# A first feed-forward turn split into token halves, with earlier loads of chunks and weights

## The chip, the cores and the metric

The kernel runs on one NeuronCore of a Trainium2 chip. The time is that of one execution on the device in microseconds (us); of several runs the median counts. A second path for inputs out of range (`slow`) is in the program and is skipped by a flag.

## What is computed

```python
f = 1.0 / (1.0 + np.exp(-f_logit))
for t in range(S):
    state = f[:, :, t, :, None] * state + np.einsum('bhd,bhe->bhde', k[:, :, t], v[:, :, t])
    y[:, :, t] = np.einsum('bhd,bhde->bhe', q[:, :, t], state)
```

In short: a gated linear attention over 4 sequences of 768 tokens with 8 heads of 48 (`state = f * state + k v`, `y = q state`); its output `x` (3072 tokens of 384) goes through `h = max(x @ w_in, 0)` and `(h * h) @ w_out`, with 2048 hidden units; and that through a soft mixture of 8 experts with 32 slots: logits `x @ phi`, a softmax over the tokens that gathers the slots, two layers per expert, and a softmax over the slots that gives the tokens back.

## The kernel before, in words

**Tiles.** The attention works on 24 chunks of 128 tokens, six to a sequence. Each chunk has a part that needs no matmul, `prep` (L142 on: the running product `ip` of the gates by four scans at L162, then `k` at L171 and `q` at L179 in that scale), and a part on PE, `chunk`: four transposes (`knat`, L193), the scores (L205) with their masks `a` (L208), the state sums (L220) with the state adds `S` (L226, L228), and the values (L243 from the state, L250 from the scores) with `y` (L254 to L259). Six small DMAs write `y` into `x` (L265, L268). A chunk is five steps of a generator, `stream`; `upto(n)` runs it to step n, so that 20 steps are a block of 512 tokens.

**Feed-forward.** Six blocks of 512 tokens go through 16 weight tiles `ff` of 128 hidden units each. For a pair (block, ff), `layer1` makes nine matmuls (three per 128 rows of the model, L118 to L120, since each operand is split into a high and a low part for one-pass products), then relu, square (L369 to L372) and the remainder `gl` on DVE (L374); `layer2` makes nine more into three banks `o`. The order of pairs is written out by hand: `TURNS` pairs blocks 0 and 1 so that weights can be split while they arrive: block 0 with tiles 0 to 3, block 1 with 0 to 8, block 0 with 4 to 15, block 1 with 9 to 15; then blocks 2 to 5 with all tiles. Between turns `put_by` saves the sums (L405, L407).

**The first turn** (block 0, tiles 0 to 3) does not split: `layer1_whole` and `layer2` use whole float weights and the whole `x`, in matmuls that the trace shows as two instructions each (L353, L384). It starts after step 23 (`FIRST`) and goes on to step 40, the end of block 1's attention; `x` of block 0 must be complete, that is, chunk 3 done.

**Weights.** `w_load` (L305) loads one tile as 64-bit numbers, 768 KB; `w_split` makes a float of it: two passes on ACT (L315, L319), a shift and a combine on DVE (L320, L321) and a last pass (L331 into `wn` for a whole tile, else L333 into `whi`); `w_parts` then splits it into high (ACT, L113) and low (DVE, L114). `x_split` does the same with `x`, by thirds of 512 columns. `WAHEAD` is the number of tiles loaded ahead.

**Queues.** All DMAs are issued by SP in one order (`g<-fkq` L136, `v` L138, `raw` L305, `x<-y`). The order on each engine is set ahead of time by the framework's scheduler from the order of the program and its priorities; each engine then goes through its list in order.

Of the kernel before, what the change touches and what calls it, by code (L numbers as in the profile page):

```python
# [18 lines left out]
HR = 64  # L19
# [38 lines left out]
class K:  # L58
# [173 lines left out]
    def values(self, i):  # L232
# [27 lines left out]
        if c == 0:  # L260
            self.x_alloc(b)
        xl = self.x[b][1].bitcast(F32)
        ts = slice(c * C, (c + 1) * C)
        for h in range(2):
            nc.sync.dma_start(out=xl[h * D : h * D + D, :, ts], in_=y[h * HR : h * HR + D, :KT])  # L265
        for h in range(2):
            for e, n, kt, o in PLACE[6 + h]:
                nc.sync.dma_start(out=xl[o : o + n, kt, ts], in_=y[h * HR + e : h * HR + e + n, KT])  # L268

# [20 lines left out]

    def x_split(self, b, kt):
        xh, xl = self.x[b]
        self.hl(xh[:, kt], xl[:, kt], xl[:, kt].bitcast(F32))

# [51 lines left out]

    def layer1_whole(self, b, ff):

        nc, fp = self.nc, self.fp
        x, w = self.x[b][1].bitcast(F32), self.whole[ff]  # L350
        o = self.ps.tile([128, 512], F32, tag="h", name="ph", bufs=2)[:, :TB]
        for kt in range(KT):
            nc.tensor.matmul(out=o, lhsT=w[:, kt * 128 : kt * 128 + 128], rhs=x[:, kt], start=kt == 0, stop=kt == KT - 1)  # L353
        r = fp.tile([128, TB], F32, tag="r", name="r", bufs=1)
        nc.scalar.activation(r, o, AF.Relu)
        g = fp.tile([128, TB], F32, tag="gl", name="g2", bufs=2)
        nc.scalar.activation(g, r, AF.Square)
        return g, None

    def layer1(self, b, ff):  # L360
        nc, fp = self.nc, self.fp
        x, w = self.x[b], self.w[ff]
        ph = self.ps.tile([128, 512], F32, tag="h", name="ph", bufs=2)
        o = ph[:, :TB]
# [4 lines left out]
        nc.scalar.activation(r, o, AF.Relu)  # L369
        gh = fp.tile([128, TB], F32R, tag="gh", name="gh", bufs=2)  # L370
        nc.scalar.activation(gh, r, AF.Square)  # L371
        nc.scalar.activation(r, r, AF.Square)  # L372
        gl = fp.tile([128, TB], F32R, tag="gl", name="gl", bufs=2)
        nc.vector.tensor_tensor(gl, r, gh.bitcast(F32), ALU.subtract)  # L374
        return gh, gl

    def layer2(self, b, ff, g, start, stop):

        if start:
            self.o[b] = [self.ps.tile([128, 512], F32, tag=f"o{t}", name=f"o{t}", bufs=1) for t in range(KT)]  # L380
        if g[1] is None:
            w = self.whole[ff][:, DM:]
            for t in range(KT):
                self.nc.tensor.matmul(out=self.o[b][t][:, :TB], lhsT=w[:, t * 128 : (t + 1) * 128], rhs=g[0], start=start, stop=stop)  # L384
            return
# [310 lines left out]
    def fast_blocks(self, main, pst, ast, wst, raw):  # L696

        def stream():
            for i in range(2):
                yield from self.prep(i)  # L700
            for i in range(NCH):
# [17 lines left out]

        st = stream()  # L720
        for _ in range(8):
            next(st)
        done = 0
        end = NCH * STEPS
# [6 lines left out]

        steps = [(b, ff) for b, f0, f1 in TURNS for ff in range(f0, f1)]
        paired = len(steps)
        steps += [(b, ff) for b in range(2, NB) for ff in range(NFF)]
# [5 lines left out]
        def target(n, b, ff):  # L740
            if n < n0:
                return min(2 * blk, max(FIRST, blk + (ff + 2) * blk // n0))
            if n < n1:
# [5 lines left out]
        def split(b):  # L749
            if b in unsplit:  # L750
                for kt in range(KT):
                    self.x_split(b, kt)
                unsplit.remove(b)

        def begin1(b, ff):
            if b == 0 and ff < WHOLE:
                return self.layer1_whole(b, ff)
            split(b)
# [6 lines left out]

        upto(FIRST)
        unsplit = list(ORDER)
        self.w_split(0, raw[0], True)
        wn = 1
        posts = iter(())  # L770
        pend = begin1(0, 0)
        wait = 0
        for n, (b, ff) in enumerate(steps):
            if n == 3:
                self.consts3()
            if wn < WHOLE or WHOLE <= n and wn < NFF:
                while len(raw) < min(NFF, wn + WAHEAD):
                    more_w()
                self.w_split(wn, raw[wn], wn < WHOLE)
                wn += 1  # L780
# [5 lines left out]
            nxt = None  # L786
            if n + 1 < len(steps):
                nxt = begin1(*steps[n + 1])
                if n0 <= n + 2 < n1:
                    part(steps[n + 2][1])  # L790
            upto(target(n, b, ff))
# [47 lines left out]
    def slow(self):  # L839
# [3 lines left out]
        with ExitStack() as main:  # L843
# [13 lines left out]
            with ExitStack() as st:  # L857
                self.pp = self.pool(st, "pp2")
                for b in range(NB):
                    self.x_alloc(b)  # L860
                    xh, xl = self.x[b]
                    self.hl(xh, xl, xT[:, :, b * TB : (b + 1) * TB])
                    for ff in range(NFF):
# [122 lines left out]
```

## Time and profile before

| | |
|---|---|
| median of 3 runs | 604.34 us (602.19 to 605.6) |
| profiled execution | 606.27 us, span 604.5 us |
| PE / DVE / ACT busy | 95% / 54% / 52% of the span |
| PE's mean granted clock | 0.989 |
| share of the chain of waits | PE 77%, DVE 7%, DMA 6%, ACT 6% |

Busy shares are means over stages. A row of an engine's list gives start and duration, and an idle time before it with the engine or DMA that ended it. [...]

### The profile page before, as it was taken

The numbers are of one execution on the slowest core, as the hardware profiler recorded it, in microseconds if no ns is written. First come the engines' busy times: TensorE is split into PE (matmuls) and PEld (weight loads), VectorE is DVE, ScalarE is ACT, GpSimd is POOL, SyncE is SP. The second block draws the span as 40 slices with busy tenths as digits, with TensorE's granted clock in tenths as the row PEclk, the third lists the DMA queues.
The fourth block names the chain that finished last, engine by engine and source line by source line (L and its number), as shares of the span: only waits on it lengthen the run. The fifth ranks groups of instructions, "written<-read, shape, count | busy, mean of one in ns | idle before, by whom it ended". The sixth has DMA issues, their size and how long they took to land.

```text
span 604.5 us, 13326 instructions
## 1 busy us (share of the span) xinstructions
PE 574.9 (95%) x5587; PEld 442.4 (73%) x5587; DVE 328.7 (54%) x688; ACT 314.8 (52%) x577; POOL 4.0 (1%) x10
## 2 busy tenths in 40 slices
PE   4899899999999999999999999999999999998993
PEld 3784467788787878778877777887788887886372
DVE  6978989999825547454464552543332322213322
ACT  5647759996635546354455354544334544442122
POOL 0000000000000000000000000000000100000000
PEclk9999979999999999999999999999999999999898
DMA  9557558421321202202211210220000745554757
GB/s 290 181 154 236 160 190 287 151 67 47 105 60 40 73 2 73 59 16 73 73 46 28 74 63 18 79 79 3 15 14 12 263 135 177 168 199 157 262 205 272
DMA packets 28324, 69.59 MB, mean 115 GB/s; under 512 B 4464, under 2 KB 17008, under 8 KB 28256
## 3 DMA queue, kind: packets, MB, share of 16 engines
q1 hardware_dynamic: 28256, 68.65, 35.8%
q8 instruction: 46, 0.75, 0.5%
q14 instruction: 22, 0.18, 0.1%
HBM read 59.20 MB, written 4.72 MB: 106 GB/s over the span
## 4 chain that ended last, share of the span: by engine, by line
PE 77%; DVE 7%; DMA 6%; ACT 6%; issue 2%; SPq 1%; ACTq 0%; DVEq 0%
PE o L118 10%; PE ph L118 9%; PE o L120 9%; PE ph L120 9%; PE ph L119 9%; PE o L119 9%; DMA g<-fkq 4%; PE psm L243 3%; DMA raw<-w 2%; DVE ip L162 2%; PE hp L591 2%; PE psm L220 2%; PE psm L205 2%; PE so L615 2%; PE o L384 1%
## 5 line engine op out<-in xcount | busy, mean ns | idle before, releaser
L374 DVE TENSOR_TENSOR gl<-r,gh 128x512 fp32r<-128x512 f32 x92 | 63.5, 690 | 119.2 <-ACT r L372 118.6
L369 ACT ACTIVATE r<-ph 128x512 f32<-128x512 f32 x92 | 54.7, 595 | 119.9 <-PE ph L120 114.9
L118 PE MATMUL o<-gh,w 128*128 128x512 f32 x276 | 112.8, 409 | 0.0
L118 PE MATMUL ph<-x,w 128*128 128x512 f32 x276 | 111.5, 404 | 0.0
L119 PE MATMUL o<-gh,w 128*128 128x512 f32 x276 | 108.0, 391 | 0.0
L120 PE MATMUL o<-gl,w 128*128 128x512 f32 x276 | 106.3, 395 | 1.8 <-DVE gl L374 1.7
L120 PE MATMUL ph<-x,w 128*128 128x512 f32 x276 | 107.8, 391 | 0.0
L119 PE MATMUL ph<-x,w 128*128 128x512 f32 x276 | 107.6, 390 | 0.0
L120 PEld LDWEIGHTS o<-gl,w 128*128 128x128 f32 x276 | 51.6, 188 | 15.7 <-DVE gl L374 4.8
L118 PEld LDWEIGHTS ph<-x,w 128*128 128x128 f32 x276 | 51.8, 188 | 14.7 <-issue 4.1
L118 PEld LDWEIGHTS o<-gh,w 128*128 128x128 f32 x276 | 51.7, 187 | 12.6 <-ACT gh L371 0.5
L120 PEld LDWEIGHTS ph<-x,w 128*128 128x128 f32 x276 | 51.8, 188 | 11.5
L371 ACT ACTIVATE gh<-r 128x512 fp32r<-128x512 f32 x92 | 58.3, 634 | 2.0
L119 PEld LDWEIGHTS ph<-x,w 128*128 128x128 f32 x276 | 51.9, 188 | 9.7
L372 ACT ACTIVATE r<-r 128x512 f32<-128x512 f32 x92 | 58.0, 630 | 1.8
L119 PEld LDWEIGHTS o<-gh,w 128*128 128x128 f32 x276 | 51.9, 188 | 9.4
L156 ACT ACTIVATE g<-g 112x512 f32<-112x512 f32 (+1 forms) x25 | 15.1, 609 | 41.8 <-DMA g<-fkq 41.8
L243 PEld LDWEIGHTS psm<-q,S 48*48 48x48 f32 (+1 forms) x704 | 27.2, 147 | 9.7 <-issue 4.6
L243 PE MATMUL psm<-q,S 48*48 48x64 f32 (+1 forms) x704 | 31.5, 244 | 2.5 <-DVE S L226 1.3
L162 DVE TENSOR_TENSOR_SCAN ip<-g,ip,big 112x128 f32<-112x128 f32 x80 | 33.4, 467 | 0.4 <-ACT g L158 0.2
L220 PEld LDWEIGHTS psm<-v,n 64*48 64x48 f32 (+1 forms) x704 | 21.3, 146 | 10.8 <-issue 5.3
L169 ACT ACTIVATE g<-ip 112x512 f32<-112x512 f32 (+1 forms) x25 | 15.3, 611 | 26.2 <-DVE ip L162 26.1
(143 smaller groups left out, 683.0 us busy)
## 6 DMA issues: line engine op xcount, KB each, us to landing
m<-m SPq DMA_DIRECT2D x26, 768.0 KB, 4.4
g<-fkq SPq DMA_DIRECT2D x23, 672.0 KB, 5.2
raw<-w SPq DMA_DIRECT2D x16, 768.0 KB, 7.1
v<-v SPq DMA_DIRECT2D x24, 192.0 KB, 3.6
g<-m SPq DMA_DIRECT2D x6, 768.0 KB, 4.5
out_dram<-ob SPq DMA_DIRECT2D x18, 256.0 KB, 3.3
x<-y SPq DMA_DIRECT2D x48, 72.0 KB, 2.8
x<-y SPq DMA_DIRECT2D x48, 16.0 KB, 1.8
```

The costliest lines, as they stand in the source:

```text
L118: mm(out=out, lhsT=sh, rhs=mh, start=start, stop=False)
L119: mm(out=out, lhsT=sl, rhs=mh, start=False, stop=False)
L120: mm(out=out, lhsT=sh, rhs=ml, start=False, stop=stop)
L156: nc.scalar.activation(f[:, s], f[:, s], AF.Exp, scale=-1.0)
L162: nc.vector.tensor_tensor_scan(ip[:, p], f[:, p], big, 1.0 if first else self.ip[:, p, C - 1 : C], ALU.mult, ALU.min)
L169: nc.scalar.activation(f[:, s], ip[:, s], AF.Ln)
L220: nc.tensor.matmul(out=pu[c][m, p], lhsT=U["n"][r, p, m], rhs=U["v"][r, hd * D : hd * D + D], start=True, stop=True)
L243: nc.tensor.matmul(out=pz[h * HR : h * HR + m, p, r], lhsT=U["S"][c][d, p * D : p * D + m], rhs=U["q"][d, p, r], start=True, stop=True)
L369: nc.scalar.activation(r, o, AF.Relu)
L371: nc.scalar.activation(gh, r, AF.Square)
L372: nc.scalar.activation(r, r, AF.Square)
L374: nc.vector.tensor_tensor(gl, r, gh.bitcast(F32), ALU.subtract)
```

## The change

1. The first turn is cut in two halves of 256 tokens. `HALVES` gives, for each of the eight pairs (half, ff), the step of the attention at which it is put in: the first half's four at steps 13 to 19, the second half's at 23 to 35. `layer1_whole` and the new `layer2_whole` work on one half; a tile's weight split comes right before its first half, with high priority. The loop over pairs starts with the second turn, at step 40.
2. `x` is laid out by chunks: for each chunk its three pieces of 128 columns lie together. The large writes of `y` into `x` become one run of 384 columns per row, `x_split` goes by chunks (four passes of 384 columns), and `layer1` reads four pieces of 128 columns per matmul.
3. In step 1 of chunk i, chunk i + 3 is loaded (before: i + 2, from i = 3 on); `v` has four buffers instead of three, and with each such load goes a weight tile while fewer than six are ahead. Chunk 3 and tiles 2 and 3 are issued before the attention starts.

```diff
-WAHEAD = 4
+WAHEAD = 6
-FIRST = 23
+HALVES = 13, 15, 17, 19, 23, 27, 31, 35
...
-        v = ap.tile([128, DM], F32, tag="v", name="v", bufs=3)
+        v = ap.tile([128, DM], F32, tag="v", name="v", bufs=4)
...
-            nc.sync.dma_start(out=xl[h * D : h * D + D, :, ts], in_=y[h * HR : h * HR + D, :KT])
+            nc.sync.dma_start(out=xl[h * D : h * D + D], in_=y[h * HR : h * HR + D, :KT])
...
-        x = self.x_room(b % 2).rearrange("p (x k t) -> p x k t", x=2, k=KT)
+        x = self.x_room(b % 2).rearrange("p (x c k t) -> p x c k t", x=2, c=NC, k=KT)
...
-    def layer1_whole(self, b, ff):
+    def layer1_whole(self, b, ff, half):
...
+        cs = slice(half * NC // 2, (half + 1) * NC // 2)
+        x, w = self.x[b][1].bitcast(F32)[:, cs], self.whole[ff]
...
+    def layer2_whole(self, b, ff, half, g):
+
+        first, last = (ff, half) == (0, 0), (ff, half) == (WHOLE - 1, 1)
...
+        ts = slice(half * TB // 2, (half + 1) * TB // 2)
+        for t in range(KT):
+            self.nc.tensor.matmul(out=self.o[b][t][:, ts], lhsT=w[:, t * 128 : (t + 1) * 128], rhs=g, start=first, stop=last)
...
-            self.mm3(o, w[:, 0, ks], w[:, 1, ks], x[0][:, kt], x[1][:, kt], kt == 0, kt == KT - 1)
+            self.mm3(o, w[:, 0, ks], w[:, 1, ks], x[0][:, :, kt], x[1][:, :, kt], kt == 0, kt == KT - 1)
...
-                    new = i + 3 if i < 2 else i + 2
-                    if j == (4 if i < 2 else 1) and i != 2 and new < NCH:
-                        self.loaded[new] = self.chunk_load(new)
-                        if new < 5:
+                    if j == 1 and 0 < i < NCH - SLOTS:
+                        self.loaded[i + SLOTS] = self.chunk_load(i + SLOTS)
+                        if len(raw) < wn + WAHEAD:
                             more_w()
...
+        self.loaded[SLOTS] = self.chunk_load(SLOTS)
+        for _ in range(2):
+            more_w()
...
-        upto(FIRST)
+
         unsplit = list(ORDER)
-        self.w_split(0, raw[0], True)
-        wn = 1
+        order = [(half, ff) for half in range(2) for ff in range(WHOLE)]
+        pend = None
+        for (half, ff), at in zip(order, HALVES):
+            upto(at)
+            if not half:
+                with self.tc.high_priority():
+                    self.w_split(wn, raw[wn], True)
+                wn += 1
+            g = self.layer1_whole(0, ff, half)
+            if pend:
+                self.layer2_whole(0, *pend)
+            pend = ff, half, g
+        upto(2 * blk)
+        wait = 0
         posts = iter(())
-        pend = begin1(0, 0)
-        wait = 0
-        for n, (b, ff) in enumerate(steps):
-            if n == 3:
+        nxt = begin1(*steps[0])
+        self.layer2_whole(0, *pend)
+        self.put_by(0)
+        pend = nxt
+        for n, (b, ff) in enumerate(steps, n0):
+            if n == n0:
                 self.consts3()
```

**The order at SP, from the weight tiles 0 and 1 on** (`raw<-w` a weight tile, `g<-fkq` and `v<-v` a chunk, `x<-y` the result of a chunk). Before:

```order
L305 DMA raw<-w 128x1536 x2
L136 DMA g<-fkq 112x1536
L265 DMA x<-y 48x3x128 x2
L268 DMA x<-y 32x128
L268 DMA x<-y 16x128
L268 DMA x<-y 32x128
L268 DMA x<-y 16x128
L138 DMA v<-v 128x384
L305 DMA raw<-w 128x1536
L136 DMA g<-fkq 112x1536
```

With the change:

```order
L304 DMA raw<-w 128x1536 x2
L136 DMA g<-fkq 112x1536
L138 DMA v<-v 128x384
L304 DMA raw<-w 128x1536 x2
L264 DMA x<-y 48x384 x2
L267 DMA x<-y 32x128
L267 DMA x<-y 16x128
L267 DMA x<-y 32x128
L267 DMA x<-y 16x128
L136 DMA g<-fkq 112x1536
L138 DMA v<-v 128x384
L304 DMA raw<-w 128x1536
```

Chunk 3's `v` and tiles 2 and 3 have moved ahead of chunk 0's results, and chunk 4 has its `v` and a tile right behind it.

**The order at DVE around chunk 1's state add** (`a` masks chunk 1's scores, `S_97` is chunk 1's first state add, `whi` a weight split, `t` and `q` belong to chunk 2's `prep`, `ip` to chunk 3's scans). Before:

```order
L171 TENSOR_TENSOR k<-g,ip 112x512
L208 TENSOR_TENSOR a<-psm,mask 128x256 x2
L228 TENSOR_TENSOR S_97<-S_96,psm 112x192
L320 TENSOR_SCALAR whi<-whi 128x768
L177 TENSOR_TENSOR t<-ip,g 112x512
L228 TENSOR_TENSOR S_98<-S_97,psm 112x192
```

With the change:

```order
L319 TENSOR_SCALAR whi<-whi 128x768
L208 TENSOR_TENSOR a<-psm,mask 128x256
L320 SCALAR_TENSOR_TENSOR whi<-raw,whi 128x768
L208 TENSOR_TENSOR a<-psm,mask 128x256
L319 TENSOR_SCALAR whi<-whi 128x768
L177 TENSOR_TENSOR t<-ip,g 112x512
L320 SCALAR_TENSOR_TENSOR whi<-raw,whi 128x768
L178 SCALAR_TENSOR_TENSOR t<-t,g 112x512
L162 SCALAR_TENSOR_TENSOR ip<-g,ip,big 112x128
L179 TENSOR_TENSOR q<-g,t 112x512
L162 SCALAR_TENSOR_TENSOR ip<-g,ip,big 112x128 x3
L228 TENSOR_TENSOR S_97<-S_96,psm 112x192
```

Two weight splits, the rest of chunk 2's `prep` and chunk 3's scans have moved ahead of the state add.

**The order at DVE up to the first `gl` of the second turn** (`xt` saves block 0's sums, `w` and `x` are remainders of splits, `S_95` chunk 8's second state add, `k` and `t` chunk 9's). Before:

```order
L407 COPY xt<-o_841 128x512
L320 TENSOR_SCALAR whi<-whi 128x768 x2
L407 COPY xt<-o_843 128x512
L321 SCALAR_TENSOR_TENSOR whi<-raw,whi 128x768
L114 TENSOR_TENSOR x<-x 128x512 x3
L333 ISA whi<-raw,whi 128x1536
L321 SCALAR_TENSOR_TENSOR whi<-raw,whi 128x768
L160 TENSOR_SCALAR g<-g 112x512
L114 TENSOR_TENSOR w<-whi,w 128x768
L333 ISA whi<-raw,whi 128x1536
L374 TENSOR_TENSOR gl<-r,gh 128x512
```

With the change:

```order
L228 TENSOR_TENSOR S_95<-S_98,psm 112x192
L114 TENSOR_TENSOR w<-whi,w 128x768
L114 TENSOR_TENSOR x<-x 128x384
L114 TENSOR_TENSOR w<-wn,w 128x768
L171 TENSOR_TENSOR k<-g,ip 112x512
L114 TENSOR_TENSOR w<-whi,w 128x768
L319 TENSOR_SCALAR whi<-whi 128x768
L177 TENSOR_TENSOR t<-ip,g 112x512
L320 SCALAR_TENSOR_TENSOR whi<-raw,whi 128x768
L319 TENSOR_SCALAR whi<-whi 128x768
L332 ISA whi<-raw,whi 128x1536
L384 TENSOR_TENSOR gl<-r,gh 128x512
```

Chunk 8's state adds and chunk 9's products stand ahead of the first `gl`, and so do more weight splits.

## Rows read from the trace of the kernel before

**Rows 1.** Busy time by stretch (columns: PE, PEld, DVE, ACT, POOL, granted clock, DMA).
```profile
0.00:18.30 18.30, 8.44 (x161) 7.34 (x163) 12.66 (x34) 9.98 (x20) 1.10 (x8) 1.00 0.87 274
18.30:86.90 68.60, 63.33 (x921) 44.23 (x917) 58.66 (x121) 43.29 (x77) 0.00 (x0) 0.95 0.60 176
...
70.00:80.00 10.00, 7.89 (x113) 4.98 (x115) 7.82 (x17) 5.35 (x10) 0.00 (x0) 0.77 0.70 213
...
0.00:99.00 99.00, 83.87 (x1136) 60.58 (x1136) 83.36 (x172) 63.16 (x114) 1.10 (x8) 0.97 0.70 213
...
100.00:120.00 20.00, 20.00 (x120) 15.77 (x119) 19.57 (x33) 19.25 (x34) 0.00 (x0) 1.00 0.47 172
```

**Rows 2.** Who waited for whom, 18.3 to 86.9 us (total, times, longest).
```profile
ACT raw L315 <- DMA raw<-w: 5.2, 3, 2.3
...
ACT g L156 <- DMA g<-fkq: 4.0, 3, 1.8
...
DVE y L259 <- PE psm L250: 3.1, 2, 1.9
```

**Rows 3.** Chain of waits that ended last (start, us, what).
```profile
30.69 7.15 DMA raw<-w
...
98.55 0.61 DVE gl L374
...
101.55 0.23 PE ph L119
...
196.27 0.66 PE psm L415 x6
```

**Rows 4.** Timeline of DVE (start, us, instruction).
```profile
19.07 0.35 DVE L228 TENSOR_TENSOR S<-S,psm 112x192 f32<-112x192 f32 x1
...
23.23 1.61 DVE L162 TENSOR_TENSOR_SCAN ip<-g,ip,big 112x128 f32<-112x128 f32 x4 [0.19 <-ACT g L158]
```

**Rows 5.** Timeline of PE, 0 to 95 us.
```profile
22.30 1.01 PE L193 MATMUL psm<-ident,k 112*128 112x112 f32 x4
...
39.32 1.01 PE L193 MATMUL psm<-ident,k 112*128 112x112 f32 x4 [0.15 <-ACT y L254]
...
45.55 4.13 PE L353 MATMUL ph<-x,wn 128*128 128x512 f32 x6
...
60.65 2.84 PE L353 MATMUL ph<-x,wn 128*128 128x512 f32 x6
...
71.76 0.55 PE L193 MATMUL psm<-ident,k 112*128 112x112 f32 x4
...
75.71 2.07 PE L384 MATMUL o<-g,wn 128*128 128x512 f32 x2
...
81.09 5.14 PE L384 MATMUL o<-g,wn 128*128 128x512 f32 x10
...
86.94 0.50 PE L118 MATMUL ph<-x,w 128*128 128x512 f32 x1
```

**Rows 6.** Timeline of PE, 96 to 131 us, chunk 8's matmuls.
```profile
110.01 0.49 PE L220 MATMUL psm<-v,n 64*64 64x48 f32 x21
...
127.15 0.97 PE L243 MATMUL psm<-q,S 48*48 48x64 f32 x26
...
128.06 0.63 PE L250 MATMUL psm<-a,v 64*48 64x64 f32 x27
```

**Rows 7.** Groups of DVE instructions, 18.3 to 99 us (busy us, mean ns).
```profile
L321 DVE SCALAR_TENSOR_TENSOR whi<-raw,whi 128x768 int32<-128x768 int32 x7 | 6.6, 949 | 0.1
...
L208 DVE TENSOR_TENSOR a<-psm,mask 128x256 f32<-128x256 f32 x14 | 5.4, 417 | 0.0
...
L177 DVE TENSOR_TENSOR t<-ip,g 112x512 f32<-112x512 f32 x7 | 4.8, 688 | 1.2 <-ACT g L170 1.0
...
L320 DVE TENSOR_SCALAR whi<-whi 128x768 int32<-128x768 int32 x8 | 4.3, 551 | 0.6 <-ACT whi L319 0.5
L228 DVE TENSOR_TENSOR S<-S,psm 112x192 f32<-112x192 f32 x12 | 4.2, 348 | 2.5 <-PE psm L220 2.5
```

More of the change, by code (lines that the diff above doesn't have):

```diff
@@ L261, in values @@
             self.x_alloc(b)
-        xl = self.x[b][1].bitcast(F32)
-        ts = slice(c * C, (c + 1) * C)
+        xl = self.x[b][1].bitcast(F32)[:, c]
         for h in range(2):
-            nc.sync.dma_start(out=xl[h * D : h * D + D, :, ts], in_=y[h * HR : h * HR + D, :KT])
+            nc.sync.dma_start(out=xl[h * D : h * D + D], in_=y[h * HR : h * HR + D, :KT])
         for h in range(2):
             for e, n, kt, o in PLACE[6 + h]:
-                nc.sync.dma_start(out=xl[o : o + n, kt, ts], in_=y[h * HR + e : h * HR + e + n, KT])
+                nc.sync.dma_start(out=xl[o : o + n, kt], in_=y[h * HR + e : h * HR + e + n, KT])
     def chunk(self, i):
@@ L289, in x_room, with x_split @@
         return self.fp.tile([128, 2 * KT * TB], F32R, tag=f"x{j}", name="x", bufs=1)
-    def x_split(self, b, kt):
+    def x_split(self, b, c):
         xh, xl = self.x[b]
-        self.hl(xh[:, kt], xl[:, kt], xl[:, kt].bitcast(F32))
+        self.hl(xh[:, c], xl[:, c], xl[:, c].bitcast(F32))
     def w_load(self, ff):
@@ L345, in w_parts @@
         self.w[ff] = t
-    def layer1_whole(self, b, ff):
+    def layer1_whole(self, b, ff, half):
         nc, fp = self.nc, self.fp
-        x, w = self.x[b][1].bitcast(F32), self.whole[ff]
-        o = self.ps.tile([128, 512], F32, tag="h", name="ph", bufs=2)[:, :TB]
+        cs = slice(half * NC // 2, (half + 1) * NC // 2)
+        x, w = self.x[b][1].bitcast(F32)[:, cs], self.whole[ff]
+        o = self.ps.tile([128, 512], F32, tag="h", name="ph", bufs=2)[:, : TB // 2]
         for kt in range(KT):
-            nc.tensor.matmul(out=o, lhsT=w[:, kt * 128 : kt * 128 + 128], rhs=x[:, kt], start=kt == 0, stop=kt == KT - 1)
-        r = fp.tile([128, TB], F32, tag="r", name="r", bufs=1)
+            nc.tensor.matmul(out=o.rearrange("p (c t) -> p c t", c=NC // 2), lhsT=w[:, kt * 128 : kt * 128 + 128], rhs=x[:, :, kt], start=kt == 0, stop=kt == KT - 1)
+        r = fp.tile([128, TB], F32, tag="r", name="r", bufs=1)[:, : TB // 2]
         nc.scalar.activation(r, o, AF.Relu)
-        g = fp.tile([128, TB], F32, tag="gl", name="g2", bufs=2)
+        g = fp.tile([128, TB], F32, tag="gl", name="g2", bufs=2)[:, : TB // 2]
         nc.scalar.activation(g, r, AF.Square)
-        return g, None
+        return g
+    def layer2_whole(self, b, ff, half, g):
+        first, last = (ff, half) == (0, 0), (ff, half) == (WHOLE - 1, 1)
+        if first:
+            self.o[b] = [self.ps.tile([128, 512], F32, tag=f"o{t}", name=f"o{t}", bufs=1) for t in range(KT)]
+        w = self.whole[ff][:, DM:]
+        ts = slice(half * TB // 2, (half + 1) * TB // 2)
+        for t in range(KT):
+            self.nc.tensor.matmul(out=self.o[b][t][:, ts], lhsT=w[:, t * 128 : (t + 1) * 128], rhs=g, start=first, stop=last)
     def layer1(self, b, ff):
@@ L363, in layer1 @@
         ph = self.ps.tile([128, 512], F32, tag="h", name="ph", bufs=2)
-        o = ph[:, :TB]
+        o = ph[:, :TB].rearrange("p (c t) -> p c t", c=NC)
         for kt in range(KT):
             ks = slice(kt * 128, kt * 128 + 128)
-            self.mm3(o, w[:, 0, ks], w[:, 1, ks], x[0][:, kt], x[1][:, kt], kt == 0, kt == KT - 1)
+            self.mm3(o, w[:, 0, ks], w[:, 1, ks], x[0][:, :, kt], x[1][:, :, kt], kt == 0, kt == KT - 1)
         r = fp.tile([128, TB], F32, tag="r", name="r", bufs=1)
-        nc.scalar.activation(r, o, AF.Relu)
+        nc.scalar.activation(r, ph[:, :TB], AF.Relu)
         gh = fp.tile([128, TB], F32R, tag="gh", name="gh", bufs=2)
@@ L380, in layer2 @@
             self.o[b] = [self.ps.tile([128, 512], F32, tag=f"o{t}", name=f"o{t}", bufs=1) for t in range(KT)]
[L381 to L385, printed above, removed]
         w = self.w[ff][:, :, DM:]
@@ L720, in fast_blocks @@
         st = stream()
+        wn = 0
         for _ in range(8):
             next(st)
+        self.loaded[SLOTS] = self.chunk_load(SLOTS)
+        for _ in range(2):
+            more_w()
         done = 0
@@ L730, in upto @@
                 done += 1
-        steps = [(b, ff) for b, f0, f1 in TURNS for ff in range(f0, f1)]
-        paired = len(steps)
+        steps = [(b, ff) for b, f0, f1 in TURNS[1:] for ff in range(f0, f1)]
+        paired = WHOLE + len(steps)
         steps += [(b, ff) for b in range(2, NB) for ff in range(NFF)]
@@ L740, in target @@
         def target(n, b, ff):
-            if n < n0:
-                return min(2 * blk, max(FIRST, blk + (ff + 2) * blk // n0))
             if n < n1:
@@ L750, in split @@
             if b in unsplit:
-                for kt in range(KT):
-                    self.x_split(b, kt)
+                for c in range(NC):
+                    self.x_split(b, c)
                 unsplit.remove(b)
         def begin1(b, ff):
-            if b == 0 and ff < WHOLE:
-                return self.layer1_whole(b, ff)
             split(b)
@@ L764, in part @@
                 self.w_parts(ff, self.whole[ff])
-        upto(FIRST)
         unsplit = list(ORDER)
-        self.w_split(0, raw[0], True)
-        wn = 1
-        posts = iter(())
-        pend = begin1(0, 0)
-        wait = 0
-        for n, (b, ff) in enumerate(steps):
-            if n == 3:
+        order = [(half, ff) for half in range(2) for ff in range(WHOLE)]
[12 more added lines that the diff above has]
+        wait = 0
+        posts = iter(())
+        nxt = begin1(*steps[0])
[4 more added lines that the diff above has]
+            if n == n0:
                 self.consts3()
-            if wn < WHOLE or WHOLE <= n and wn < NFF:
+            if wn < NFF:
                 while len(raw) < min(NFF, wn + WAHEAD):
                     more_w()
-                self.w_split(wn, raw[wn], wn < WHOLE)
+                self.w_split(wn, raw[wn])
                 wn += 1
@@ L786, in fast_blocks @@
             nxt = None
[L787 to L790, printed above, removed]
+            if n + 1 - n0 < len(steps):
+                nxt = begin1(*steps[n + 1 - n0])
+                if n + 2 < n1:
+                    part(steps[n + 2 - n0][1])
             upto(target(n, b, ff))
```

2 lines of the change are left out of this document (1 added, 1 removed).

## The prediction

> **What bounds the kernel now.** I read the busy times by stretch first, then who waited for whom, then the chain of waits, then the timelines of VectorE (DVE) and TensorE (PE) over the first 100 us. The stretches show two regimes. Up to 18.3 us DVE works 12.66 us, and up to 86.9 us another 58.66 of 68.6. From about 99 us PE is full: 20.00 of 20 us between 100 and 120, while DVE and ScalarE (ACT) are nearly full too, 19.57 and 19.25 [rows 1]. So what PE has not done by 99 us lengthens the program, and later work of DVE is hidden as long as it keeps up.
>
> What ends the first regime is DVE. The chain of waits leaves DVE at the second `gl` of the second turn, at 98.55 for 0.61 us, and stays on PE from there, with a matmul of 512 columns every 0.23 us [rows 3]. Up to 99.0 us DVE was busy 83.36 us, so it was idle for 15.6: 5.6 before 18.3, 9.9 from there to 86.9, and almost nothing after [rows 1]. The waits between 18.3 and 86.9 say why. ACT waited 5.2 us for raw weights and 4.0 for `fkq` chunks; DVE itself waited 3.1 for the matmuls of L250 [rows 2]. One such load stands in the chain with 7.15 us [rows 3]. These are waits that earlier loads can remove.
>
> TensorE's level matters as well. The four transposes of a chunk took 1.01 us at 22.30 and 0.55 at 71.76; six matmul instructions of the first turn took 4.13 us at 45.55 and 2.84 at 60.65 [rows 5]. [...] Between 70 and 80 us, with PE busy 7.89 of 10, the mean granted clock was 0.77 [rows 1], and at 75.71 two instructions took 2.07 us, as against 5.14 for the ten from 81.09. These ran just ahead of the second turn, which began at 86.94 [rows 5].
>
> **The change, part by part.** *Loads.* Weight tiles 2 and 3 are issued right behind chunk 3, and from chunk 5 on each chunk comes one chunk sooner. They join a full queue: 274 GB/s up to 18.3 us [rows 1], 5.0 MB in all. The v of chunk 3 and two tiles are 1.7 MB more and land by about 25 us at that rate. I take the waits for loads after that as gone. The gain is not 9.2 us, since those were waits of ACT; it is at most what DVE idled, 9.9 us.
>
> *Order on DVE.* Here lies the price. The splits of the first tiles have high priority and are now put in before chunk 2 is finished, so they stand ahead of chunk 1's state add. Before, that add ran at 19.07 [rows 4], right behind the mask products. Now two shifts (0.55), two combines (0.95), three products of chunk 2 (0.69 each) [rows 7] and four scans (1.61) [rows 4] come first, 6.7 us as listed, about 6.0 without the 0.08 by which neighbours overlap (the add at 19.07 is listed for 0.35, and the next starts 0.28 later). That makes 25.1 us. PE's values of chunk 1 wait for it, and its transposes for chunk 2 move from 22.30 [rows 5] to about 27.9. [...] A chunk took 6.2 us there (39.32 to 45.55 [rows 5]); with 6.2 to 8 for chunks 2 and 3 they end at about 42.7, and the DVE work in the order up to there, at the listed durations less overlap, leaves 4.9 us idle after 18.3.
>
> *Order before the second turn.* More DVE work stands ahead of the second `gl`: 2 state adds (0.35), 2 mask products (0.42), 2 products (0.69) and a small add (at most that), 1 weight remainder and 4 passes of two more splits (all as the combine, 0.95) and 2 shifts (0.55) [rows 7]: 0.7 + 0.8 + 2.1 + 4.8 + 1.1 = 9.5, less 14 overlaps of 0.08, 8.4 us. It is chunk 8's attention and two more tiles. DVE's work up to the second `gl` becomes 83.4 + 8.4 = 91.8 us. In return PE has done the rest of chunk 8 by then, about 2.3 us (0.49 for two thirds of L220, 0.97 for L243 and 0.57 for L250 behind it [rows 6], part of the last still open). Without loss the second `gl` may thus end at 99.2 + 2.3 = 101.5, which leaves 9.7 us of idle time.
>
> *Sum.* Idle: 5.6 before 18.3, where the order is the same; 4.9 to 42.7; and 2 from there on, where splits fill most gaps (bounds: none, and the old share of 9.9 in 68.6). 91.8 + 12.5 = 104.3, that is 2.8 us late.
>
> *Level at the second turn.* The first turn's last matmuls now stand ahead of chunk 7's values, so PE has only attention between them and the second turn, and I expect it low again when that begins. Bounds: nothing, if DVE is later still, and two chunks at twice their time, 2 x 2.8 = 5.6 us (nearly half of 6.2 each). I take 1.3, the 4.13 less the 2.84 [rows 5], since a run of wide matmuls raises it again. **Sum: about 4 us slower.**
>
> [...]
>
> *At nothing.* The x splits take four passes of 384 columns for three of 512, the same columns. Relu and square come as 16 instructions instead of 8 on half the columns; 8 more of even 0.6 us fit in the 25 us that ACT idles in the 68.6 [rows 1]. Matmuls read x in four pieces of 128 columns: six transposes of 128 columns took 0.66 us [rows 3], 0.11 each, and 0.47 is what 512 took (2.84 / 6 [rows 5]), so short pieces cost no more than their columns; were it 1%, the 828 matmuls of layer 1 at 0.23 would give 1.9 us. The writes of x have longer runs and as many issues; what they gain, they gain once, under 2 us, behind DVE. Later stages keep their order.
>
> **Rivals.** *One, the cover holds (faster).* With the loads early DVE never idles after 18.3: the second `gl` ends at 91.8 + 5.6 = 97.4, 4.1 us early, and the time is 600. For it: after 43 us many splits are ready to fill gaps. Against it: from 25 to 43 us PE at its low level is in the way, and part of DVE's own waits was for PE [rows 2]. It is faster by more than the measurement can tell only if DVE idles less than about 1.1 us after 18.3. *Two, it evens out:* 9.7 us idle in all, 604. *Three, slower by more:* PE is low for two chunks (5.6), or DVE idles at its old share: 91.8 - 12.7 = 79.1 us of work takes 92.5 at 58.66 / 68.6, the second `gl` ends at 110.8, 9.3 us late. That is 610 to 613.5. *Four, the change doesn't do what it says:* the halves are in the program sooner, but run no sooner, since they queue behind chunks 2 and 3 on PE: 42.7 here, 45.55 before [rows 5]. If the gain of the loads just pays for the order, this is rival two.
>
> **How the numbers follow.** The profiled execution took 606.27 us (span 604.5); 4 more are 610.3. The runs have a median of 604.34, 1.9 below it, so I forecast 608.3. A measurement of this kernel can tell about 0.5%, 3 us. Chances: forecast 0.42, rival three 0.13, two and four 0.28, one 0.17. The forecast's lower edge and the upper edge of rival two trade about equal shares across the 3 us, and some 0.02 of the forecast falls below it: slower 0.53, same 0.30, faster 0.17. The range goes from rival one's 600 to rival three's 613.5.
>
> **What would show it.** Right: ACT hardly waits for raw weights before 80 us; chunk 1's state add near 25 us; DVE's longest gap near 29 to 33 us, behind PE; first-turn matmuls from about 43 us; the second turn's first matmul after 90 us and its second `gl` near 104, with PE full from there. Wrong: the state add still near 20 us, a second turn before 86 us, under 3 us of DVE idle time after 18.3, or gaps on PE after 110 us.

## The result, and the profile of the changed kernel

The changed kernel takes 612.38 us in the median of its runs (610.79 to 613.61), the kernel before beside it 604.3; the ratio is 1.0135, with a 95% interval from 1.0093 to 1.0177. It is slower, by some 8 us where 4 were forecast. Its profiled execution took 613.61 us with a span of 611.8, 7.3 us longer than that of before.

Busy time by stretch of the changed kernel, in the columns of [rows 1]:

```profile
0.00:18.30 18.30, 8.34 (x159) 7.23 (x161) 12.58 (x34) 9.89 (x20) 1.10 (x8) 1.00 0.94 294
18.30:86.90 68.60, 58.42 (x1002) 47.62 (x999) 60.43 (x124) 46.89 (x90) 0.00 (x0) 0.95 0.66 202
0.00:106.80 106.80, 83.68 (x1277) 68.25 (x1277) 91.33 (x188) 70.99 (x134) 1.10 (x8) 0.94 0.72 228
90.00:100.00 10.00, 9.01 (x73) 7.19 (x72) 8.85 (x18) 6.05 (x12) 0.00 (x0) 0.68 0.85 305
100.00:120.00 20.00, 20.00 (x96) 15.27 (x95) 19.25 (x29) 19.61 (x35) 0.00 (x0) 1.00 0.53 179
```

PE is full from 100 us here too, but before that there is more for DVE: 91.33 us up to 106.8, the end of the second `gl`, instead of 83.36 up to 99.0 [rows 1]. The timeline of DVE has the places that the prediction named:

```profile
25.18 0.33 DVE L228 TENSOR_TENSOR S<-S,psm 112x192 f32<-112x192 f32 x1
...
30.70 0.76 DVE L208 TENSOR_TENSOR a<-psm,mask 128x256 f32<-128x256 f32 x2 [1.22 <-PE psm L205]
...
99.50 0.56 DVE L319 TENSOR_SCALAR whi<-whi 128x768 int32<-128x768 int32 x1 [1.15 <-ACT whi L318]
...
101.33 0.69 DVE L384 TENSOR_TENSOR gl<-r,gh 128x512 fp32r<-128x512 f32 x1 [0.41 <-ACT r L382]
...
106.09 0.69 DVE L384 TENSOR_TENSOR gl<-r,gh 128x512 fp32r<-128x512 f32 x1
```

The state add of chunk 1 went from 19.07 [rows 4] to 25.18, and the second `gl` ends at 106.78 (106.09 and 0.69) instead of 99.16 (98.55 and 0.61 [rows 3]), 7.6 us later. The timeline of PE beside it (before: [rows 5]):

```profile
25.56 1.65 PE L243 MATMUL psm<-q,S 48*64 48x64 f32 x26 [4.47 <-DVE S L228]
...
28.09 1.01 PE L193 MATMUL psm<-ident,k 112*128 112x112 f32 x4
...
42.11 4.30 PE L353 MATMUL ph<-x,wn 128*128 128x256 f32 x12
...
88.35 0.66 PE L220 MATMUL psm<-v,n 64*64 64x48 f32 x16 [1.68 <-DVE a L208]
...
93.40 0.79 PE L118 MATMUL ph<-x,w 128*128 128x512 f32 x1
93.99 0.63 PE L119 MATMUL ph<-x,w 128*128 128x512 f32 x1
94.42 0.63 PE L118 MATMUL ph<-x,w 128*128 128x512 f32 x1
...
96.41 0.39 PE L118 MATMUL ph<-x,w 128*128 128x512 f32 x1
96.64 0.40 PE L119 MATMUL ph<-x,w 128*128 128x512 f32 x1
```

PE waits 4.47 us for that add. The first turn starts at 42.11 instead of 45.55, the second at 93.40 instead of 86.94, and it starts at the low level: 0.42 us from one matmul to the next, and 0.23 from 96.41 on. The granted clock was 0.50 of full speed from 89.6 to 96.4 us and 1.00 from there to 106.8, so 0.68 in the mean between 90 and 100.

The second `gl` is a mark in DVE's list more than a gate of PE's. From the first matmul of the second turn to the second `gl` PE has no idle time, neither before (from 86.94) nor now (from 93.40), and it waits for that `gl` 0.18 us before and not at all now. Its row behind the second `gl` before:

```profile
99.21 0.96 PE L120 MATMUL o<-gl,w 128*128 128x512 f32 x3 [0.18 <-DVE gl L374]
```

PE's idle time lies ahead of the second turn, 23.1 us there instead of 15.1: 4.47 at the add, and 3.2 from 86.7 to 91.0 us at mask products and state adds of chunk 8 that stand behind weight splits in DVE's list. Who waited for whom, 18.3 to 86.9 us (before: [rows 2]):

```profile
PE psm L243 <- DVE S L228: 5.8, 3, 4.5
...
DVE a L208 <- PE psm L205: 2.8, 3, 1.2
ACT raw L314 <- DMA raw<-w: 2.4, 1, 2.4
...
ACT g L156 <- DMA g<-fkq: 1.3, 1, 1.3
```

The loads keep ACT for 3.7 us instead of 9.2, and waits of PE and DVE for each other have come in.

Where the 7.3 us arise is read from the posts, the adds and copies in which DVE takes over a finished block. The first row of the first block's and of the last block's, before and after:

```profile
188.83 1.37 DVE L426 TENSOR_TENSOR xt<-xt,o 128x512 f32<-128x512 f32 x2 [1.99 <-PE o L120]
...
548.91 0.69 DVE L430 COPY xt<-o 128x512 f32<-128x512 f32 x1 [0.59 <-PE o L120]
```
```profile
193.02 1.37 DVE L431 TENSOR_TENSOR xt<-xt,o 128x512 f32<-128x512 f32 x2 [1.95 <-PE o L120]
...
556.28 0.69 DVE L435 COPY xt<-o 128x512 f32<-128x512 f32 x1 [0.59 <-PE o L120]
```

The first post is 4.2 us late. The second `gl` was 7.6 late, but from there PE comes to the first post in 3.4 us less (193.02 - 106.78 = 86.2 us, instead of 188.83 - 99.16 = 89.7). Of these, 2.2 are work that PE no longer has to do there (85.85 us busy instead of 88.06), since chunk 8 is done; the other 1.2 are waits, above all one of 1.13 us for a `gl` at 160.16, which PE had there before. The other 3.2 us come between these two posts, which took 360.1 us and now take 363.3, in a stretch where the order of PE is the same. Busy time of this stretch, before and then in the changed kernel:

```profile
188.80:549.00 360.20, 359.51 (x3158) 285.63 (x3158) 157.24 (x335) 175.37 (x323) 2.85 (x2) 1.00 0.25 77
```
```profile
193.00:556.30 363.30, 360.76 (x3157) 285.16 (x3157) 157.25 (x339) 176.63 (x327) 2.86 (x2) 1.00 0.25 75
```

PE idles 2.5 us there instead of 0.7. So there are two losses to explain.

### The profile page after: what moved, and what is told of

The parts are those of the page before. It is cut to its first block, busy times and chain, and to the rows that moved or that the text cites. A ratio compares the mean times of both kernels' runs of the same rounds, so it can differ in the third digit from the quotient of the medians.

```text
span 611.8 us, 13452 instructions
## 1 busy us (share of the span) xinstructions
PE 573.7 (94%) x5635; PEld 447.6 (73%) x5635; DVE 329.0 (54%) x694; ACT 318.0 (52%) x591; POOL 4.0 (1%) x10
## 2 busy tenths in 40 slices
DMA packets 23716, 69.59 MB, mean 114 GB/s; under 512 B 4464, under 2 KB 12400, under 8 KB 23648
## 4 chain that ended last, share of the span: by engine, by line
PE 70%; DVE 12%; DMA 7%; ACT 7%; issue 3%; SPq 0%; DVEq 0%; ACTq 0%
PE o L118 9%; PE ph L118 9%; PE o L120 8%; PE ph L120 8%; PE ph L119 8%; PE o L119 8%; DMA g<-fkq 5%; PE psm L243 3%; DVE ip L162 3%; PE hp L596 2%; PE so L620 2%; PE psm L205 2%; PE psm L250 2%; PE psm L220 1%; PE psm L420 1%
## 5 line engine op out<-in xcount | busy, mean ns | idle before, releaser
L120 PEld LDWEIGHTS o<-gl,w 128*128 128x128 f32 x276 | 51.6, 188 | 15.6 <-DVE gl L384 4.7
L169 ACT ACTIVATE g<-ip 112x512 f32<-112x512 f32 (+1 forms) x25 | 15.3, 613 | 32.9 <-DVE ip L162 32.3
L208 DVE TENSOR_TENSOR a<-psm,mask 128x256 f32<-128x256 f32 x48 | 18.3, 416 | 17.9 <-PE psm L205 17.9
```

The lines of the kernel that those rows point to most:

```text
L120: mm(out=out, lhsT=sh, rhs=ml, start=False, stop=stop)
L169: nc.scalar.activation(f[:, s], ip[:, s], AF.Ln)
L208: nc.vector.tensor_tensor(a[:, h], pa[h], self.mask.unsqueeze(1).to_broadcast([128, NP, HC]), ALU.mult)
```

## The experiments

The columns of this table are, for each profiled execution: DVE's busy time up to the end of the second `gl`; that end; what DVE idled up to it; the first post; the time from there to the last block's post ("first to last"). The last two are the median of the runs and the ratio to the runs of before beside them.

| kernel | DVE busy | second gl ends | idle | first post | first to last | median | ratio (95%) |
|---|---|---|---|---|---|---|---|
| before | 83.6 | 99.2 | 15.6 | 188.8 | 360.1 | 604.3 | 1 |
| changed | 91.3 | 106.8 | 15.5 | 193.0 | 363.3 | 612.4 | 1.0135 (1.0093 to 1.0177) |
| layout alone | 88.4 | 104.9 | 16.5 | 192.2 | 360.3 | 609.5 | 1.0076 (1.0055 to 1.0097) |
| changed, old layout | 90.1 | 104.5 | 14.4 | 191.3 | 361.6 | 610.9 | 1.0090 (1.0058 to 1.0121) |
| loads alone | 87.6 | 105.6 | 18.0 | 193.1 | 359.9 | 609.2 | 1.0081 (1.0051 to 1.0110) |
| changed, no priority | 93.2 | 107.3 | 14.1 | 193.4 | 361.8 | 610.8 | 1.0092 (1.0063 to 1.0122) |
| changed, old loads | 100.3 | 115.3 | 15.0 | 200.3 | 362.4 | 618.6 | 1.0252 (1.0220 to 1.0285) |
| changed, wide matmuls | 91.3 | 104.0 | 12.7 | 196.1 | 361.7 | 615.1 | 1.0176 (1.0153 to 1.0200) |
| before, additions early | 90.8 | 106.1 | 15.3 | 194.7 | 359.9 | 612.6 | 1.0161 (1.0120 to 1.0203) |
| before, additions late | 83.6 | 98.7 | 15.1 | 187.7 | 360.3 | 604.8 | 1.0010 (0.9990 to 1.0030) |
| before, shifted | 83.0 | 97.0 | 14.0 | 186.3 | 361.9 | 606.6 | 1.0048 (1.0024 to 1.0072) |
| changed, shifted | 92.0 | 106.5 | 14.5 | 193.2 | 360.6 | 608.6 | 1.0075 (1.0052 to 1.0099) |

How finely the first columns can be read is seen in three executions whose DVE order is the same up to the second `gl` (before, additions late, before shifted): their first posts lie 2.5 us apart.

**The layout alone.** To the kernel before:

```diff
-        xl = self.x[b][1].bitcast(F32)
-        ts = slice(c * C, (c + 1) * C)
+        xl = self.x[b][1].bitcast(F32)[:, c]
...
-        x = self.x_room(b % 2).rearrange("p (x k t) -> p x k t", x=2, k=KT)
+        x = self.x_room(b % 2).rearrange("p (x c k t) -> p x c k t", x=2, c=NC, k=KT)
...
-            self.mm3(o, w[:, 0, ks], w[:, 1, ks], x[0][:, kt], x[1][:, kt], kt == 0, kt == KT - 1)
+            self.mm3(o, w[:, 0, ks], w[:, 1, ks], x[0][:, :, kt], x[1][:, :, kt], kt == 0, kt == KT - 1)
...
```

> The kernel before, with x laid out by chunks alone (writes of x in longer runs, four splits of 384 columns, layer 1 reading x in pieces of 128 columns); loads and first turn as before. Theory one, the whole loss is made before the second turn by the order on VectorE: same time as before, 604 within 2 us, and the second gl of the second turn near 99 us. Theory two, some 3 us of the loss come after 234 us, where the new writes of x stand beside the loads of fkq, behind which ScalarE waits with its relus: 607, with fkq loads of 5.5 to 6.7 us where 5.0 were usual, and lateness that grows between 234 and 360 us.

Neither theory held. The time is 4.4 us up, but the loss is made ahead of the first post, not after 234 us: first to last post takes 360.3. Its busy time, and PE's timeline at the start of its second turn:

```profile
0.00:104.90 104.90, 84.06 (x1173) 61.10 (x1173) 88.39 (x183) 68.18 (x122) 1.10 (x8) 0.90 0.74 221
```
```profile
89.51 0.50 PE L118 MATMUL ph<-x,w 128*128 128x512 f32 x1 [2.39 <-ACT x L113]
...
93.03 0.63 PE L119 MATMUL ph<-x,w 128*128 128x512 f32 x1
...
93.89 0.63 PE L118 MATMUL ph<-x,w 128*128 128x512 f32 x1
```

DVE has 4.8 us more to do ahead of the second `gl`, though its work is the same but for x splits in four passes instead of three, on the same columns: with another shape of the x splits the scheduler put the DVE passes of one more weight tile, and part of chunk 8, in front. PE waits 2.39 us for an x split, and from about 90 us on the turn runs at the low level, with 0.42 us from one matmul to the next until 96.87. That matmuls read x in pieces costs next to nothing: the matmuls `ph<-x,w` took 390 to 404 ns in the mean before and 392 to 406 in the changed kernel, where they read the same pieces.

**The changed kernel with the old layout** (the lines above reversed; the first turn reads half a row):

```diff
-        cs = slice(half * NC // 2, (half + 1) * NC // 2)
-        x, w = self.x[b][1].bitcast(F32)[:, cs], self.whole[ff]
+        hs = slice(half * TB // 2, (half + 1) * TB // 2)
+        x, w = self.x[b][1].bitcast(F32)[:, :, hs], self.whole[ff]
```

> The changed kernel with x laid out as before (the halves of the first turn take 256 tokens of each row of x). Theory one: 612, as the changed kernel. Theory two: about 609, with the posts after block 1 late by 4 us and no more.

610.9, between the 609 and the 612 of the two theories. The first post is 1.8 us sooner than in the changed kernel, and 1.5 of the 3.2 late microseconds are left, so the layout is not what causes these.

**The loads alone.** To the kernel before:

```diff
-WAHEAD = 4
+WAHEAD = 6
...
-                    new = i + 3 if i < 2 else i + 2
-                    if j == (4 if i < 2 else 1) and i != 2 and new < NCH:
-                        self.loaded[new] = self.chunk_load(new)
+                    if j == 1 and 0 < i < NCH - SLOTS:
+                        self.loaded[i + SLOTS] = self.chunk_load(i + SLOTS)
...
```

> The kernel before with the earlier loads alone (chunk 3 and two weight tiles ahead of the attention, each later chunk one sooner, six tiles ahead); first turn whole and x laid out as before. If ScalarE's waits for loads (5.2 us for raw weights, 4.0 for fkq) were what idled VectorE, half or more of its 9.9 us of idle time after 18.3 us goes: second gl at 94 to 96 us, 600 to 602. If they hid behind VectorE's other work: 604, second gl near 99. If the loads in the full queue push back something that was in time: 606 or more.

609.2, the third case in time, but by another way. Of ACT's waits for loads between 18.3 and 100 us those of `raw` itself are gone, and these are left:

```profile
ACT y L254 <- DMA raw<-w: 2.9, 1, 2.9
...
ACT g L156 <- DMA g<-fkq: 0.5, 1, 0.5
```

They were 9.2 us before, and yet DVE has 4.0 us more to do ahead of the second `gl`, and idles 2.4 us more:

```profile
0.00:105.60 105.60, 85.31 (x1177) 61.97 (x1178) 87.60 (x180) 67.87 (x120) 1.10 (x8) 0.98 0.75 226
```

With the tiles there sooner, most passes of one more tile, two mask products and a state add stand ahead of it.

**No priority.** To the changed kernel:

```diff
-                with self.tc.high_priority():
-                    self.w_split(wn, raw[wn], True)
+                self.w_split(wn, raw[wn], True)
```

> The changed kernel with the splits of the first four tiles at ordinary priority. Theory one, the splits ahead of chunk 1's state add cost 4.9 us of VectorE's time behind TensorE: the state add is back near 20 us, chunk 2's transposes near 23, TensorE's wait of 4.5 us at 25.6 is gone, and the second gl comes 3 to 4 us sooner, near 103: 608 to 609. Rival, the work ahead of the second turn alone decides (8.4 us more of it): VectorE idles elsewhere instead, second gl near 106, 612.

The first half of theory one came true and its consequence didn't:

```profile
20.24 0.35 DVE L228 TENSOR_TENSOR S<-S,psm 112x192 f32<-112x192 f32 x1
...
106.57 0.69 DVE L384 TENSOR_TENSOR gl<-r,gh 128x512 fp32r<-128x512 f32 x1
```

The state add is back near 20 us, PE no longer waits for it, and its idle time ahead of the second turn falls from 23.1 to 20.6 us. But the second `gl` comes no sooner. The test is not clean: DVE idles 1.4 us less up to there, and without the priority 1.9 us more work stands ahead. So, by this sum, about 1.4 of the 7.6 us are the delay's.

In all of these DVE's idle time up to the second `gl` is 14 to 18 us, while its work there goes from 83.6 to 93.2. That gave the next theory: the price is the work that stands ahead, whatever brings it there.

**The changed kernel with the old loads** (the diff of the loads alone, reversed in the changed kernel):

```diff
-WAHEAD = 6
+WAHEAD = 4
...
-        self.loaded[SLOTS] = self.chunk_load(SLOTS)
-        for _ in range(2):
-            more_w()
```

> The changed kernel with the loads as before (four tiles ahead, chunk 3 and the next tiles later, three buffers of v). Theory now: what decides is the VectorE work that stands ahead of the second gl of the second turn in the order. Summed from the durations of single instructions less overlap it is 82.2 us in the kernel before (605.2 measured), 86.2 with the early loads alone (609.2), 87.2 with the new layout alone (609.5), 89.2 and 90.4 in the changed kernel with the old and the new layout (610.9, 612.4), 91.7 without priority (610.8): about 0.8 us of time for each us. Here it is 99.7, eight tiles split ahead instead of three or five: second gl at 113 to 116, 617 to 621. Rival, the early loads cost by themselves (a full queue): 608 to 609, the change without them.

618.6, as the theory had it, from the order alone:

```profile
0.00:115.30 115.30, 87.77 (x1296) 70.05 (x1297) 100.28 (x200) 78.27 (x145) 1.10 (x8) 0.94 0.70 218
```

By themselves the earlier loads cost 4 to 5 us; within the change they save 6 to 7. The parts do not add up; each also changes the order that the scheduler makes.

**Additions on VectorE, early and late.** To the kernel before, six additions that nobody reads; early, they read the new x and stand ahead of the second turn's first `gl`; late, they read its fourth `gl`:

```diff
+            if n == n0 + -1:
+                with self.tc.high_priority():
+                    d = self.wr.tile([128, TB], F32, tag="extra", name="extra", bufs=1)
+                    for _ in range(2):
+                        for kt in range(KT):
+                            x = self.x[1][1][:, kt].bitcast(F32)
+                            nc.vector.tensor_tensor(d, x, x, ALU.add)
```
```diff
+            if n == n0 + 3:
+                with self.tc.high_priority():
+                    d = self.wr.tile([128, TB], F32, tag="extra", name="extra", bufs=1)
+                    for _ in range(6):
+                        x = pend[1].bitcast(F32)
+                        nc.vector.tensor_tensor(d, x, x, ALU.add)
```

> The kernel before with six additions of 128x512 on VectorE (0.61 us each) that nobody reads, put by priority right ahead of the second turn's first gl: 3.7 us, and one more tile's split that the order then also puts ahead; 89.6 us stand ahead of the second gl instead of 82.2. Theory (work ahead of the second gl is the price): second gl 4 to 7 us later, 103 to 106, and 608.5 to 611. Rival (VectorE's sum of work until 160 us or its waits are the price, not the place): as much as the next kernel, or nothing, 605 to 607.

> The kernel before with the same six additions right behind the fourth gl of the second turn; 82.2 us ahead of the second gl, as before. Theory: 605 to 606, within 1 us of the kernel before, since TensorE is full from 99 us on. Rival (the sum counts): as much slower as the kernel with the early additions, 608 or more.

Early 612.6, late 604.8. Busy time up to the second `gl`, early and then late:

```profile
0.00:106.10 106.10, 83.28 (x1155) 60.66 (x1156) 90.78 (x185) 67.53 (x119) 1.10 (x8) 0.94 0.70 214
```
```profile
0.00:98.80 98.80, 83.31 (x1137) 60.61 (x1137) 83.61 (x173) 63.48 (x114) 1.10 (x8) 0.97 0.70 212
```

The same 4.1 us of work (six of 0.68) costs 8.7 us in the one place (with the split and two mask products that it draws ahead, 7.2 us of work) and nothing that can be measured in the other. The early one is 1.6 us dearer than expected. PE's timeline shows where it pays:

```profile
93.87 0.79 PE L120 MATMUL ph<-x,w 128*128 128x512 f32 x1 [5.14 <-DVE x L114]
```

The additions stand ahead of the last x splits as well, and it is for such a split, 12 us ahead of the second `gl`, that PE waits; then it goes on at the low level, with 0.43 us from one matmul to the next.

**Wide matmuls ahead of the second turn.** To the changed kernel:

```diff
+        for _ in range(12):
+            po = self.ps.tile([128, 512], F32, tag="h", name="warm", bufs=2)
+            self.nc.tensor.matmul(out=po, lhsT=self.whole[WHOLE - 1][:, :128], rhs=self.whole[WHOLE - 1][:, :512], start=True, stop=True)
         nxt = begin1(*steps[0])
```

> The changed kernel with twelve matmuls of 512 columns that nobody reads, in the program ahead of the second turn, so that TensorE has wide work shortly before it. The term of the level was 1.3 us: if it holds, the first matmuls of the second turn come 0.23 us apart instead of 0.43, and the time is 1 us less than the changed kernel's, 611. If the added matmuls (0.47 us each at full level, twice that at the low one) stand in the way of the chunks, 613 to 615. If the level costs nothing since VectorE ends last, 612.

```profile
83.63 7.99 PE L789 MATMUL warm<-wn 128*128 128x512 f32 x18
91.54 0.50 PE L118 MATMUL ph<-x,w 128*128 128x512 f32 x1
...
106.72 0.55 PE L193 MATMUL psm<-ident,k 112*128 112x112 f32 x4
```

The level held: after 93.67 the turn's matmuls follow at 0.23 us, and the second `gl` ended 2.8 us sooner than in the changed kernel. But the added matmuls take 10.0 us of PE, and chunk 8, whose transposes ran at 84.56 there, now comes at 106.72, behind the second `gl`, with the rest of its work on a PE that is full. The first post is 3.1 us later, and the time is 615.1. So the second `gl` is not the whole measure: what PE has done by then counts as well. The level by itself has no price from this run.

**The late loss.** Of the kernels so far, the five with halves took 361.6 to 363.3 us from first to last post, the five without 359.9 to 360.3. In the changed kernel PE waits for ACT there, and ACT stands behind a load of `fkq`. The timelines of ACT and PE before, and then in the changed kernel:

```profile
341.75 0.63 ACT L156 ACTIVATE g<-g 112x512 f32<-112x512 f32 x1 [4.77 <-DMA g<-fkq]
...
343.83 0.85 PE L487 MATMUL psm<-xf,dn 128*32 128x384 f32 x8
```
```profile
349.09 0.63 ACT L156 ACTIVATE g<-g 112x512 f32<-112x512 f32 x1 [6.16 <-DMA g<-fkq]
...
350.69 0.85 PE L492 MATMUL psm<-xf,dn 128*32 128x384 f32 x8 [0.83 <-ACT n L195]
```

DMA of the changed kernel from 342.4 to 349.0 us, the time of that load (queue: packets, MB, share; then issue, KB, us to landing):

```profile
q8 instruction: 1, 0.02, 1.4%
...
g<-fkq SPq DMA_DIRECT2D x1, 672.0 KB, 6.6
```

A packet of instructions fell into the load, which took 6.6 us instead of 5.2. On the whole run there are 46 such packets with 0.75 MB, 16 KB each. From the first of them, at 16.5 us, to the 44th, at 593.6, the kernel before has 10920 matmul instructions and weight loads on PE, 254 for each of the 43 steps from packet to packet. (The kernel with 256 of them more than the one before, the last of this section, has 47 packets.) The halves add 48 matmul instructions and 48 weight loads on PE, so the packets might only have moved. Two kernels move them by other means:

```diff
+            for _ in range(24):
+                po = self.ps.tile([128, 512], F32, tag="h", name="tiny", bufs=2)
+                self.nc.tensor.matmul(out=po[:1, :1], lhsT=self.big, rhs=self.big, start=True, stop=True)
             self.attention_state(self.ap)
```

(the kernel before; in the changed kernel 40 instead of 24).

> The kernel before with 24 matmuls of one column at the very start, where TensorE waits anyway, that nobody reads: as many more instructions of TensorE as the changed kernel has. The five kernels with halves lose 1.5 to 3.2 us more between 189 and 549 us, the other five (the kernel before among them) 0.2 at most; in the first, fkq loads of 6.5 to 6.7 us near 340 us had a packet of the queue of instructions 1.5 to 2 us after their issue. Theory: these packets bring TensorE's instructions, and their place against the loads moves with the number of instructions: second gl at 98 to 99 as before, a load of over 6 us near 340, the stretch from 189 to 549 us 1.5 to 3 us longer, 606 to 608. Rival (the halves do it otherwise): that stretch as before, 360.1, and 605.

> The changed kernel with 40 such matmuls at the start, so that its number of instructions of TensorE stands against the kernel before's by one whole packet (16 KB, some 256 instructions, of which these and their weight loads are 160 and the halves 96). Theory: the loads near 340 us take 5.0 to 5.4 us again, the stretch between the posts of the first and the last block is 360 instead of 363.3, and the time is 609 to 610, with the second gl near 106 as in the changed kernel. Rival: 363 there and 612.

Timelines of ACT and PE, and the DMA of that load (334.2 to 341.0 us), of the kernel before with the shift:

```profile
340.94 0.63 ACT L156 ACTIVATE g<-g 112x512 f32<-112x512 f32 x1 [6.13 <-DMA g<-fkq]
...
342.53 0.85 PE L487 MATMUL psm<-xf,dn 128*32 128x384 f32 x8 [0.81 <-ACT n L195]
```
```profile
q8 instruction: 1, 0.02, 1.8%
...
g<-fkq SPq DMA_DIRECT2D x1, 672.0 KB, 6.6
```

and of the changed kernel with the shift, where no packet of instructions falls into this load:

```profile
346.61 0.63 ACT L156 ACTIVATE g<-g 112x512 f32<-112x512 f32 x1 [4.68 <-DMA g<-fkq]
```
```profile
g<-fkq SPq DMA_DIRECT2D x1, 672.0 KB, 5.1
```

Both came out as expected, the second a little faster: the kernel before now loses 1.9 us from first to last post and has the long load and PE's wait of 0.8 us; the changed kernel gets 2.7 of its 3.2 us back there and is 3.8 us faster in the median, 608.6. The first is the clean one: apart from the 24 matmuls, DVE, ACT, GpSimd and SP go through the same lists in the same order as before, to the end. In the second the scheduler moved the order a little too, though its second `gl` and its first post lie within 0.3 us of where they were.

The posts of the third and the fourth block, on either side of this load, show its price. From one to the other it takes 84.8 to 85.1 us in the six kernels where the load took 5.1 to 5.3 us, 85.6 in the one where it took 5.9, and 86.2 to 87.0 in the five where it took 6.4 to 6.6. So 2.1 us of the changed kernel's 3.2, and 1.3 to 1.8 in the four others, come with the place of the packets and not with what the halves compute. The rest of the 3.2 arises between the second and the third block's posts (87.1 us instead of 85.9); no run here takes that apart. None of the kernels beats the one before.

## Why the prediction was right, and where not

**The forecast** was 608.3, slower, in a range from 600 to 613.5. The 612.4 lie in the range, at its upper end, on the forecast's side of no change. Its shifted form, which is without most of the late loss, takes 608.6.

**What bounds it** held in the main: work of DVE ahead of the second turn is paid for, and later work of DVE is hidden. The additions show it, early and late. But PE is full from the start of the second turn, 12.2 us ahead of the end of the second `gl` before and 13.4 now; the chain of waits stepped to DVE there over a wait of 0.18 us. That does the sum little harm, since the distance is nearly the same.

**Work ahead of the second `gl`:** 91.8 us forecast, 91.3 measured. This is the step that carries the result, and the one that was derived from the order; the instructions added ahead are the ones that it listed, and x splits in smaller passes.

**Idle time:** 12.5 forecast, 15.5 measured; here the sum failed. To 18.3 us it is 5.7 (5.6 forecast), from there to 43 us 4.0 (4.9), but from 43 us on 5.7 instead of 2. "I take the waits for loads after that as gone" was wrong for 3.7 us of ACT's up to 86.9 us, all of them after 70. But what failed is the thought behind it, that their going saves DVE idle time: in the kernel with the loads alone two thirds of them are gone, and DVE idles more. In all kernels but two the idle time is 14 to 16.5 us, so the second `gl` ends at about 15 us plus the work ahead of it.

**"Here lies the price"**, the state add at 25.1 us: the add came at 25.18 and the transposes at 28.09 as forecast, DVE's gap of 1.22 us behind PE at 30.70, the first turn at 42.11. But it is hardly the price: without the priority the add is at 20.24, DVE idles only 1.4 us less, and the second `gl` is as late.

**The credit for chunk 8** was 2.3 us and is 2.2 of PE's busy time; the 1.2 us of PE's waits that went behind the second `gl` had no term. The kernel with wide matmuls agrees with the credit: where chunk 8 falls behind, the time grows although the second `gl` is sooner.

**The level** was put on top with 1.3 us; it is inside the second `gl`'s lateness, five of the turn's matmuls and six of chunk 8's in the 3.0 us from 93.40 to 96.41, about half of which, 1.5 us by this estimate, the full level would have saved. The granted clock was 0.50 there, up to 96.4 us, as it was from 75.5 to 82.3 in the kernel before. The loss was near the 1.3 us taken, not the upper bound of 5.6.

**Together:** 2.8 + 1.3 = 4.1 us forecast at the first post, and 7.6 - 3.4 = 4.2 measured. That it fits so well is luck in part: 3 us more of idle time stand against the 1.3 us of a level that was put on top and lies inside, half a microsecond less of work, and 1.2 us of waits that went. And the 3.2 us that came after it were not in the sum at all.

**"At nothing"** failed for the layout. The columns are the same, as the working said, and reading in pieces is all but free. But the shape of the splits changed DVE's order, and alone it costs 4.4 us. **"Later stages keep their order"** is true of PE, and they still took 3.2 us longer: the step had no term for what else moves when instructions are added, here the packets that bring them.

**The rivals.** One, the cover, and two, the even sum, fell with the idle time. Three gave 610 to 613.5, where the result is, but by its second condition only in part: DVE idled as much in all as before, not at its old share of a longer time (9.3 us late), and PE was not low for two chunks. Four held in its first half: the halves ran behind chunks 2 and 3, from 42.11 (42.7 forecast). But the gain of the loads that was to pay for the order isn't there.

## What to carry to other kernels

Where one engine ends a stage, sum up its work that stands ahead of what the next engine waits for, and don't count on shorter waits: here they stayed at 14 to 16.5 us in ten kernels of twelve, and 4 us of work, with 3 that it drew ahead, cost 8.7 in front of that place and nothing behind it. Look in the next engine's own list where that place is; the end of a chain of waits can hang on 0.2 us. An edit to loads or to a tile's shape is also an edit to the order that a scheduler makes, so compare the orders first and don't expect the effects of parts to add up. And before a difference of half a per cent is put down to an edit, add some instructions that do nothing: if that moves the time as much, the edit's own work need not be the cause.

## What the runs showed of the hardware that was not expected

Packets of instructions share the DMA with the loads. In the stretch from 187 to 350 us of all these executions, a load of 672 KB took 6.4 to 6.6 us in five of the six cases where such a packet came 1 to 2.5 us behind its issue (5.2 in the sixth), 4.6 to 5.9 where it came within 0.5 us of it, and 4.4 to 5.3 where it came 3 us or more behind or not at all. The five are all the same load, near 340 us; so for the other loads this is not shown. One long load, in front of an ACT that works in order, stopped a full PE for 0.8 us. Which of the 16 DMA engines the packet met was not looked at. Of the 3.1 us by which the stretch of the changed kernel is longer (363.3 instead of 360.2), 1.8 are PE's idle time; how the rest comes to lie in its busy time stays open.

That no gain of the new writes of x is to be seen is the other surprise: they go in longer runs (23716 DMA packets in the changed kernel instead of 28324, for the same bytes), and the layout alone made the kernel slower. What the writes gain by themselves is not shown, since DVE's order changed with them.
